# Loading wq in four transfers of spaced rows, and other cuts of wo, in a decode kernel

## The chip, the cores and the metric

The kernel runs on one core of a Trainium2 chip. Its time is the device time of one execution in microseconds (us); the median of several executions is given. A profile is one execution taken by the hardware profiler.

## The reference

One token passes through grouped-query attention over a long cache and through a SwiGLU block, and a gate mixes the two. All inputs are bf16.

```python
# x [1,1,512]; wq [512,4096]; wo [4096,512]; K and V [1,8,32768,128]; w_gate, w_up [512,1792]; w_down [1792,512]
g = sigmoid((x * gate_w).sum(-1, keepdims=True))
q = (x @ wq)                                   # 32 heads of 128, four heads share one of the 8 K/V heads
p = softmax((q @ k^T) * 128 ** -0.5)           # over 32768 positions
a = (p @ v) @ wo
b = (silu(x @ w_gate) * (x @ w_up)) @ w_down
out = g * a + (1 - g) * b
```

K and V are 64 MB each, so 148 MB are read for very little arithmetic.

## The kernel before

All loads are issued by the sync engine (SP) on one queue, in an order written out by hand: wq, then the rows x and gate_w, w_gate, w_up, then K and V head by head into five pages of SBUF as they come free, then w_down, and last wo. Sixteen DMA engines serve that queue.

**wq** (line 307) comes as one transfer. Partition p of the page `PG_Q` receives rows 4p to 4p+3 of wq, which lie together in memory: 32 KB a partition, 128 partitions. (In this document "a row of wq" is one such 32 KB row of a partition.) TensorE waits for it (line 458, `sem_q` at 16) and then multiplies x with it.

**K and V** are streamed by a loop over the 8 K/V heads. TensorE transposes pieces of K into PSUM (`emit_fill`, line 337), VectorE copies them to SBUF, TensorE makes scores (line 349), ScalarE takes exponentials, and TensorE multiplies with V (line 406). SP waits for pages to come free before it issues the next load.

**wo** (lines 325 to 329) comes in five transfers. Partition p receives 32 rows of wo, and a "row block" j is the j-th of these on all partitions (1 KB a partition, 128 KB in all). `WO_CUTS` says which row blocks a transfer brings: 16, 8, 4, 2 and 2.

**The end** has two ways to multiply with a row block. `emit_strip` makes one matmul of 512 columns into one of four PSUM rows of `ps_c`. Four such partial rows must later be added: ScalarE copies `ps_c` to SBUF as `part` (line 763), and TensorE adds its four rows with the selecting vector `sel4` in fp32 (line 760). `emit_rows` makes four matmuls of 128 columns, straight into the final place `ps_d`. Row blocks below `WO_ROWS` (24) go by strips, on top of the strips of w_down; the others go by rows. The first piece of wo is used inside `emit_end` (line 557); the other four and the sum stand in the loop at lines 756 to 760. VectorE then casts the result (line 765) and SP stores it (line 768).

Of the kernel before, what the change touches and what calls it, by code (L numbers as in the profile page):

```python
# [12 lines left out]
def bass_gated_mix__gqa_block_cached__swiglu_ffn__decode_kernel(  # L13
# [16 lines left out]
    DH = A_k_cache.shape[3]  # L30
    H = A_wq.shape[1] // DH
# [5 lines left out]
    KC = D // 128  # L37
# [13 lines left out]
    LAG = 2  # L51
    STEP = 16
    WOJ = H * DH // 128
    SCALE = float(DH) ** -0.5
    assert UPG == STEP and UPP % NKT == 0 and UPP % NST == 0
    assert KC * H * DH <= PAGE and 2 * KC * F <= PAGE and WOJ * NOUT <= PAGE
    WO_CUTS = [0, 16, 24, 28, 30, 32]
    WO_ROWS = 24
    OC = NOUT // 128
    FS = F // 4  # L60

# [10 lines left out]
    PG_Q = PG_V  # L72
# [5 lines left out]
    with ExitStack() as es:  # L78
        def S_(name):
            return es.enter_context(nc.semaphore(name))  # L80
# [5 lines left out]
        sem_q = S_("s_q")  # L86
        sem_f = S_("s_f")
        sem_wo = [S_(f"s_wo{i}") for i in range(len(WO_CUTS) - 1)]
        sem_ld_x = S_("s_ld_x")
# [42 lines left out]
        sem_part = S_("s_part")  # L132
# [4 lines left out]
        def T(name, shape, dt):  # L137
            return es.enter_context(nc.sbuf_tensor(name, shape, dt))
# [11 lines left out]
        sel4 = T("sel4", [128, 16], FP32)  # L150
# [7 lines left out]
        page = T("page", [128, NPG, PAGE], BF16)  # L158
# [12 lines left out]
        oTs = T("oTs", [128, H], BF16)  # L171
        O2a = T("O2a", [128, WOJ], BF16)
        O2 = T("O2", [128, WOJ], BF16)
        res_row = T("res_row", [128, 128], BF16)
# [14 lines left out]
        M_O0 = M_T0 + FC  # L189
        M_X0 = M_O0 + WOJ  # L190
        M_G0 = M_X0 + KC
# [16 lines left out]
        part = acc[:, :, :].rearrange("p q d -> p (q d)")  # L208

        def vrows(pg):  # L210
            return page[:, pg, :].rearrange("p (r d) -> p r d", d=DH)

        wq_v = page[:, PG_Q, 0 : KC * H * DH].rearrange("p (c n) -> p c n", c=KC)
        wgu = page[:, PG_F, 0 : 2 * KC * F].rearrange("p (w c f) -> p w c f", w=2, c=KC)
        wo_v = page[:, PG_X, 0 : WOJ * NOUT].rearrange("p (j n) -> p j n", j=WOJ)
        qall = qblk[:, :].rearrange("p (g e c) -> p g e c", e=2, c=2 * HPG)

        def emit_strip(pe, w, vec, j, start, stop):
            c = j % NSTRIP
            return pe.matmul(  # L220
                ps_c[32 * c : 32 * c + 1, :],
                vec[:, j : j + 1],
                w[:, j, :],
                start=start,
                stop=stop,
                skip_group_check=True,
            )

        def emit_rows(pe, lhsT, rhs, start, stop):
            for oc in range(OC):  # L230
                ins = pe.matmul(  # L231
                    ps_d[32 * oc : 32 * oc + 1, :],
                    lhsT,
                    rhs[:, oc * 128 : (oc + 1) * 128],
                    start=start,
                    stop=stop,
                    skip_group_check=True,
                )
            return ins

        def emit_wo(pe, k):
            pe.wait_ge(sem_wo[k], 16)
            for j in range(WO_CUTS[k], WO_CUTS[k + 1]):
                if j < WO_ROWS:
                    ins = emit_strip(pe, wo_v, O2, j, False, j >= WO_ROWS - NSTRIP)
                else:
                    ins = emit_rows(
                        pe, O2[:, j : j + 1], wo_v[:, j, :], j == WO_ROWS, j == WOJ - 1
                    )
            if WO_CUTS[k + 1] == WO_ROWS:  # L250
                ins.then_inc(sem_pe_part, 1)
            return ins
# [4 lines left out]
        with nc.Block("main") as block:  # L257
# [12 lines left out]
            @block.sync  # L270
            def _(sp):
                def load_k(g):
                    lo = PG_A if g % 2 else PG_B
                    dst = page[:, lo : lo + NB, :].rearrange("p b (r d) -> p b r d", d=DH)
                    src = A_k_cache[0, g, :, :].rearrange("(p b r) d -> p b r d", b=NB, r=R)
                    if g > 1:
                        sp.wait_ge(sem_fill, UPG * (g - 1) + UPP)
                        sp.dma_start(
                            dst.rearrange("p b r d -> p (b r d)"),
                            src.rearrange("p b r d -> p (b r d)"),  # L280
                        ).then_inc(sem_k[0], 16)
                        return
                    for b in range(NB):
                        first = lo + b == PG_B
                        if g and first:
                            sp.wait_ge(sem_fill, UPP)
                        sp.dma_start(dst[:, b, :, :], src[:, b, :, :]).then_inc(
                            sem_k[0] if first else sem_k1 if g else sem_k[1], 16
                        )

                def load_v(g):
                    src = A_v_cache[0, g, :, :].rearrange("(p b r) d -> p b r d", b=NB, r=R)
                    if g < G - 1:
                        if g:
                            sp.wait_ge(sem_v_free, STEP * (g + 1))
                        else:
                            sp.wait_ge(sem_pe_h, 1)
                        sp.dma_start(
                            page[:, PG_V : PG_V + NB, :].rearrange("p b n -> p (b n)"),
                            src.rearrange("p b r d -> p (b r d)"),  # L300
                        ).then_inc(sem_v, 16)
                        return
                    for b in range(NB):
                        sp.wait_ge(sem_fill, UPG * (G - 1 + b))
                        sp.dma_start(vrows(PG_L[b]), src[:, b, :, :]).then_inc(sem_vl[b], 16)

                sp.dma_start(wq_v, A_wq.rearrange("(p c) n -> p c n", c=KC)).then_inc(sem_q, 16)  # L307
                sp.dma_start(x_row[0:1, :], A_x[0, :, :]).then_inc(sem_ld_x, 16)  # L308
                sp.dma_start(gw_row[0:1, :], gate_w.unsqueeze(0)).then_inc(sem_ld_g, 16)
                for w, src in enumerate((B_w_gate, B_w_up)):  # L310
                    sp.dma_start(  # L311
                        wgu[:, w, :, :], src.rearrange("(p c) f -> p c f", c=KC)
                    ).then_inc(sem_f, 16)
                load_k(0)
                for g in range(1, G):
                    load_k(g)
                    if g == 2:
                        sp.wait_ge(sem_ident, 2)
                        sp.dma_start(out_rows, ident[SEL, :]).then_inc(sem_out, 16)
                    load_v(g - 1)  # L320
                load_v(G - 1)
                sp.dma_start(
                    wd[:, :, :], B_w_down.rearrange("(p j) n -> p j n", j=FC)
                ).then_inc(sem_ld_wd, 16)
                sp.wait_ge(sem_v_free, STEP * G)
                src = A_wo.rearrange("(p j) n -> p j n", j=WOJ)
                for k, s in enumerate(sem_wo):
                    a, b = WO_CUTS[k], WO_CUTS[k + 1]
                    sp.dma_start(wo_v[:, a:b, :], src[:, a:b, :]).then_inc(s, 16)  # L329

            @block.tensor
            def _(pe):
# [103 lines left out]
                def emit_start():  # L436
# [18 lines left out]
                    ins.then_inc(sem_pe_x, 1)  # L455
                    pe.wait_ge(sem_pz, 2)
                    pe.wait_ge(sem_dve_x, 1)
                    pe.wait_ge(sem_q, 16)
                    for t in range(QT):
                        for c in range(KC):  # L460
                            for k in range(NSTRIP):
                                n = (t * NSTRIP + k) * QN
# [60 lines left out]
                    for n, sem in enumerate((sem_v_free, sem_red)):  # L523
                        c = M_P0 + HPG * n
# [34 lines left out]
                with pe.Fori(0, 2, 1) as turn:  # L559
                    with pe.If(turn > 0):  # L560
                        emit_end()
                    with pe.If(turn < 1):
                        emit_start()

            @block.scalar
            def _(act):
# [10 lines left out]
                with act.Fori(0, G * STEP, STEP) as i:  # L577
# [5 lines left out]
                    for b in range(NB):  # L583
                        bank = R - odd if b else odd
                        for h in range(HPG):
# [4 lines left out]
                                bias=nbias[:, h : h + 1],  # L590
                                scale=SCALE,
                                accum_out=esum[:, b, h : h + 1],
# [5 lines left out]
            def _(dve):  # L598
# [108 lines left out]
                with dve.Fori(0, G * STEP, STEP) as i:  # L707
                    for n in range(UPG + 1):
# [28 lines left out]
                    dve.tensor_scalar(  # L737
                        nbias[:, :], ps_m[:, M_B0 : M_B0 + HPG], -SCALE, None, op0=ALU.mult
                    ).then_inc(sem_nbias, STEP)
# [13 lines left out]
                dve.tensor_copy(O2[:, :], ps_m[:, M_O0 : M_O0 + WOJ]).then_inc(sem_dve_O2, 1)  # L753

        pe, act, dve, sp = nc.tensor, nc.scalar, nc.vector, nc.sync
        for k in range(1, len(sem_wo)):
            ins = emit_wo(pe, k)
            if WO_CUTS[k] == WO_ROWS:
                pe.wait_ge(sem_part, 1)
                emit_rows(pe, sel4[:, 0:1], part, False, False)  # L760
        ins.then_inc(sem_pe_sum, 1)
        act.wait_ge(sem_pe_part, 1)
        act.activation(part, ps_c, ACT.Copy).then_inc(sem_part, 1)
# [34 lines left out]
```

## Time and profile before

| | before |
|---|---|
| median of 3 runs | 351.08 us (350.98 to 351.13) |
| the profiled execution | 351.06 us, of which its span is 349.7 us |
| mean granted TensorE clock | 0.838 |
| PE (matmuls) busy | 259.8 us, 74% of the span |
| VectorE busy | 186.9 us, 53% |
| ScalarE busy | 33.4 us, 10% |
| DMA, share of 16 engines | 98.4% |
| DMA, mean rate | 424 GB/s for 148.22 MB |

The span runs from the first to the last instruction of the core; the time of an execution is a little longer. Engines are named PE (TensorE matmuls), PEld (its weight loads), DVE (VectorE), ACT (ScalarE), POOL (GpSimd) and SP; SPq is SP's DMA queue. A share of busy time is an average over stages with different limits, so it only says where to look. A line of the profile such as `L307` names a line of the kernel before.

### The profile page before, as it was taken

What the parts mean: (1) busy time and instruction counts of PE and PEld (TensorE: products, weight loads), DVE (VectorE), ACT (ScalarE), POOL (GpSimd) and SP (SyncE); (2) the same over time, 40 slices, a digit from 0 to 9 for tenths busy, and PEclk for the clock granted to TensorE, in tenths of its full rate; (3) what the DMA queues carried; (4) which work ended last, traced back from release to release, by engine and by line L of the source; (5) the groups of instructions that cost most, each with busy time, mean ns of one, the idle gap of its engine ahead of it and who ended that gap; (6) DMA issues with size and microseconds to landing.
All of it is one profiled execution on the core that took longest, in us unless ns stands there. A gap on an engine that the chain in (4) does not pass through costs nothing.

```text
span 349.7 us, 8785 instructions
## 1 busy us (share of the span) xinstructions
PE 259.8 (74%) x3891; PEld 217.9 (62%) x3891; DVE 186.9 (53%) x236; ACT 33.4 (10%) x143; POOL 0.4 (0%) x6
## 2 busy tenths in 40 slices
PE   1355993899649970999669992999179983999485
PEld 1124993898349950997369942996179843995231
DVE  4144994698129920697139910994149811893110
ACT  1002000300210003000210003000300003000400
POOL 0000000000000000000000000000000000000000
PEclk9975998799859995799659986999659975998875
DMA  8999999999999999999999999999999999999995
GB/s 320 429 449 420 433 423 453 452 412 435 457 405 450 412 442 465 412 427 442 412 465 412 427 442 427 450 412 435 472 405 435 442 412 465 412 397 435 421 420 216
DMA packets 4059, 148.22 MB, mean 424 GB/s; under 512 B 466, under 2 KB 468, under 8 KB 852
## 3 DMA queue, kind: packets, MB, share of 16 engines
q1 hardware_dynamic: 4052, 148.12, 98.4%
q8 instruction: 6, 0.10, 0.1%
q14 instruction: 1, 0.01, 0.0%
HBM read 148.11 MB, written 0.00 MB: 423 GB/s over the span
## 4 chain that ended last, share of the span: by engine, by line
DMA 61%; PE 34%; issue 2%; DVE 1%; SPq 1%; DVEq 0%
DMA page<-in_A_k_cache_dram 55%; PE pst L337 25%; PE ps_sc L349 6%; DMA page<-in_A_wo_dram 6%; PE ps_o L406 2%; DVE ktT L711 1%; PE ps_sc L231 0%; SPq L311 0%; SPq L329 0%; DVE pmaxf L719 0%; PE ps_m L390 0%; PE ps_m L386 0%; SPq L307 0%; SPq L308 0%; DVE res_row L765 0%
## 5 line engine op out<-in xcount | busy, mean ns | idle before, releaser
L711 DVE COPY ktT<-pst 128x2048 bf16<-128x2048 bf16 x128 | 153.1, 1221 | 65.2 <-PE pst L337 61.0
L337 PE MATMUL pst<-ident_f,page 128*128 128x128 f32 x1024 | 145.9, 296 | 41.2 <-DMA page<-in_A_k_cache_dram 39.6
L337 PEld LDWEIGHTS pst<-ident_f,page 128*128 128x128 f32 x1024 | 124.3, 153 | 45.9 <-DMA page<-in_A_k_cache_dram 40.3
L349 PE MATMUL ps_sc<-qcur,ktT 128*128 128x8 bf16 x2048 | 64.1, 166 | 6.4 <-DVE ktT L711 6.4
L349 PEld LDWEIGHTS ps_sc<-qcur,ktT 128*128 128x128 bf16 x2048 | 63.7, 96 | 8.1 <-DVE ktT L711 7.1
L406 PE MATMUL ps_o<-page,ET 128*16 128x512 bf16 x512 | 38.4, 467 | 3.5 <-ACT ET L586 3.5
L406 PEld LDWEIGHTS ps_o<-page,ET 128*16 128x16 bf16 x512 | 14.3, 105 | 23.9 <-issue 12.2
L586 ACT ACTIVATE ET<-ps_sc,nbias 128x128 bf16 x64 | 23.9, 555 | 52.2 <-DVE nbias L737 52.2
L579 ACT ACTIVATE acc<-ps_o 128x512 f32<-128x512 f32 x8 | 4.8, 597 | 221.3 <-PE ps_o L406 217.3
L729 DVE TENSOR_REDUCE gm<-ps_m 4x1 f32<-4x128 f32 x8 | 2.2, 279 | 40.8 <-PE ps_m L386 40.8
L586 ACT ACTIVATION_READ_ACCUMULATOR ET<-ps_sc,nbias 128x1 f32 x64 | 18.2, 285 | 0.0
L719 DVE TENSOR_REDUCE pmaxf<-ps_sc 128x4 f32<-128x512 f32 x16 | 11.0, 686 | 8.4 <-PE ps_sc L349 8.4
L427 PE MATMUL ps_m<-sel,acc 128*128 128x4 f32 x64 | 8.4, 255 | 1.8 <-ACT acc L579 1.6
L427 PEld LDWEIGHTS ps_m<-sel,acc 128*128 128x128 f32 x64 | 7.7, 191 | 2.5 <-ACT acc L579 2.2
L390 PE MATMUL ps_m<-diag,ones_f 4*128 4x4 f32 x16 | 4.0, 315 | 6.9 <-DVE diag L733 6.9
L390 PEld LDWEIGHTS ps_m<-diag,ones_f 4*128 4x128 f32 x16 | 3.5, 270 | 8.4 <-issue 8.4
L696 DVE RECIPROCAL rS<-ps_m 128x4 f32<-128x4 f32 x9 | 1.6, 183 | 11.0 <-PE ps_m L427 11.0
L448 PE MATMUL ps_m<-ones_bf,x_row 1*128 1x1 bf16 x4 | 0.3, 172 | 9.3 <-DMA x_row<-in_A_x_dram 9.3
L418 PEld LDWEIGHTS ps_m<-esum,ones_f 128*128 128x128 f32 x32 | 4.2, 190 | 3.5 <-issue 3.5
L448 PEld LDWEIGHTS ps_m<-ones_bf,x_row 1*128 1x128 bf16 x4 | 0.2, 114 | 9.6 <-DMA x_row<-in_A_x_dram 9.6
L220 PE MATMUL ps_sc<-page,O 128*1 128x512 bf16 x24 | 2.7, 592 | 3.3 <-DMA page<-in_A_wo_dram 3.3
L418 PE MATMUL ps_m<-esum,ones_f 128*128 128x4 f32 x32 | 4.9, 258 | 0.0
(70 smaller groups left out, 52.5 us busy)
## 6 DMA issues: line engine op xcount, KB each, us to landing
page<-in_A_k_cache_dram SPq DMA_DIRECT2D x4, 4096.0 KB, 34.3
page<-in_A_v_cache_dram SPq DMA_DIRECT2D x2, 4096.0 KB, 27.2
page<-in_A_wq_dram SPq DMA_DIRECT2D x1, 4096.0 KB, 13.5
page<-in_A_wo_dram SPq DMA_DIRECT2D x1, 2048.0 KB, 18.5
page<-in_B_w_gate_dram SPq DMA_DIRECT2D x1, 1792.0 KB, 16.7
page<-in_B_w_up_dram SPq DMA_DIRECT2D x1, 1792.0 KB, 20.6
wd<-in_B_w_down_dram SPq DMA_DIRECT2D x1, 1792.0 KB, 21.0
page<-in_A_wo_dram SPq DMA_DIRECT2D x1, 1024.0 KB, 20.7
```

Source lines behind the costliest of these rows:

```text
L220: return pe.matmul(ps_c[32 * c : 32 * c + 1, :], vec[:, j : j + 1], w[:, j, :], start=start, stop=stop, skip_group_check=True,)
L337: ins = pe.transpose(pst[u % NST][:, k * 128 : (k + 1) * 128], kv[:, n * 128 : (n + 1) * 128], ident_f[:, :],)
L349: ins = pe.matmul(ps_sc[b][:, col : col + 2 * HPG], kt[:, k, e, :], qcur[:, e, :], start=(e == 0), stop=(e == 1),)
L390: pe.matmul(ps_m[:, M_B0 : M_B0 + HPG], ones_f[0:HPG, :], diag[:, :], start=True, stop=True,).then_inc(sem_b, STEP)
L406: ins = pe.matmul(ps_o[32 * c : 32 * c + RQ * HPG, :], ET[:, n : n + RQ, :].rearrange("p n h -> p (n h)"), v[:, k * RQ : (k + 1) * RQ, :], ...
L418: pe.matmul(ps_m[:, M_S0 : M_S0 + HPG], ones_f[:, :], esum[:, b, :], start=(b == 0), stop=(b == NB - 1),)
L427: ins = pe.matmul(ps_m[:, M_P0 : M_P0 + HPG], acc[:, q, :], sel4[:, q * HPG : (q + 1) * HPG], start=(q == 0), stop=(q == RQ - 1),)
L579: act.activation(part, ps_o[:, :], ACT.Copy).then_inc(sem_acc, STEP)
L586: act.activation(ET[:, b * R : (b + 1) * R, h], sc[:, h, bass.ds(bank, R)], ACT.Exp, bias=nbias[:, h : h + 1], scale=SCALE, accum_out=esum ...
L711: dve.tensor_copy(ktT[:, n % NKT, :], pst[n % NST][:, :].bitcast(BF16)).then_inc(sem_cp, 1)
L719: dve.tensor_reduce(pmaxf[:, b, :], sc, AX.X, ALU.max).then_inc(sem_d, 1)
L729: dve.tensor_reduce(gm[:, :], ps_m[0:HPG, M_A0 : M_A0 + 128], AX.X, ALU.max).then_inc(sem_d, STEP - 2)
```

## The change

wq is no longer one transfer but four on the same queue: the first takes every 8th row from row 0, the second every 8th row from row 4, the third every 4th row from row 2, the fourth every 2nd row from row 1. These are 16, 16, 32 and 64 rows of 32 KB. TensorE waits for all four. wo comes in pieces of 16, 9, 4, 2 and 1 row blocks. Only the first piece goes by strips; the sum of the four strips is placed ahead of the row matmuls of the other four pieces, and it is now the first matmul into `ps_d`.

```diff
-    WO_CUTS = [0, 16, 24, 28, 30, 32]
-    WO_ROWS = 24
+    WQ_ROWS = ((0, 8), (4, 8), (2, 4), (1, 2))
+    WO_CUTS = [0, 16, 25, 29, 31, 32]
+    WO_ROWS = WO_CUTS[1]
...
                     ins = emit_rows(
-                        pe, O2[:, j : j + 1], wo_v[:, j, :], j == WO_ROWS, j == WOJ - 1
+                        pe, O2[:, j : j + 1], wo_v[:, j, :], False, j == WOJ - 1
                     )
...
-                sp.dma_start(wq_v, A_wq.rearrange("(p c) n -> p c n", c=KC)).then_inc(sem_q, 16)
+                wq_d = page[:, PG_Q, 0 : KC * H * DH]
+                wq_s = A_wq.rearrange("(p c) n -> p (c n)", c=KC)
+                for first, step in WQ_ROWS:
+                    sp.dma_start(wq_d[first::step, :], wq_s[first::step, :]).then_inc(sem_q, 16)
...
-                    pe.wait_ge(sem_q, 16)
+                    pe.wait_ge(sem_q, 16 * len(WQ_ROWS))
...
         pe, act, dve, sp = nc.tensor, nc.scalar, nc.vector, nc.sync
+        pe.wait_ge(sem_part, 1)
+        emit_rows(pe, sel4[:, 0:1], part, True, False)
         for k in range(1, len(sem_wo)):
             ins = emit_wo(pe, k)
-            if WO_CUTS[k] == WO_ROWS:
-                pe.wait_ge(sem_part, 1)
-                emit_rows(pe, sel4[:, 0:1], part, False, False)
```

## The prediction

> **What bounds the kernel now.** I read the page first: its engine shares and 40 slices, then its DMA rows. After those came SP's timeline for the first 3 us, a table of short stages over the first 13 us, the timeline of the last 7 us, and the chain of waits.
>
> From the page, the DMA row of the 40 slices, the queue row, and the landing of wq:
>
> ```profile
> DMA  8999999999999999999999999999999999999995
> ...
> q1 hardware_dynamic: 4052, 148.12, 98.4%
> ...
> page<-in_A_wq_dram SPq DMA_DIRECT2D x1, 4096.0 KB, 13.5
> ```
>
> The sixteen DMA engines are at 98.4% of the span. PE is busy 74% of it, but the chain that ended last gives DMA 61%. Only the first slice (8) and the last (5) are open. Time can therefore be won or lost in three ways: the DMA engines start sooner or later, some transfer runs below the full rate, or the work behind the last landing changes. The full rate is the page's mean of 424 GB/s, 26.5 GB/s an engine. A row of wq is 4096 KB / 128 = 32 KB, so it takes an engine 32.8 KB / 26.5 = 1.24 us.
>
> The start, SP's timeline (start us, length us):
>
> ```profile
> 0.74 0.38 SPq L307 DMA_DIRECT2D page<-in_A_wq_dram  x1
> 1.18 0.31 SPq L308 DMA_DIRECT2D x_row<-in_A_x_dram  x1
> ```
>
> and the table of stages (the last number is GB/s; a packet is booked in the stage in which it starts, which is why a share can pass 1):
>
> ```profile
> 0.00:1.50 1.50, 0.00 (x0) 0.00 (x0) 0.57 (x5) 0.77 (x1) 0.44 (x6) 1.00 0.00 0
> 1.50:2.50 1.00, 0.00 (x0) 0.00 (x0) 0.86 (x6) 0.51 (x1) 0.00 (x0) 1.00 1.79 492
> 2.50:3.50 1.00, 0.98 (x4) 0.93 (x4) 0.71 (x2) 0.00 (x0) 0.00 (x0) 1.00 0.16 66
> 3.50:4.50 1.00, 0.24 (x2) 0.00 (x0) 0.84 (x2) 0.00 (x0) 0.00 (x0) 1.00 1.16 492
> ```
>
> 492 KB are 15 rows of wq. Fifteen engines began their first row in 1.5 to 2.5 us, and the next fifteen rows began in 3.5 to 4.5. The first row of each engine thus took about 2.0 us, not 1.24: the start loses some 0.75 us an engine beside the latency of the issue.
>
> The end, timeline (PE = matmuls, PEld = weight loads):
>
> ```profile
> 342.39 1.73 PE L220 MATMUL ps_sc<-page,O 128*1 128x512 bf16 x16 [2.61 <-DMA page<-in_A_wo_dram]
> 344.81 1.02 PE L220 MATMUL ps_sc<-page,O 128*1 128x512 bf16 x8 [0.69 <-DMA page<-in_A_wo_dram]
> 345.88 0.60 ACT L763 ACTIVATE acc<-ps_sc 128x512 f32<-128x512 f32 x1 [8.53 <-PE ps_sc L220]
> 346.08 0.60 PE L231 MATMUL ps_sc<-page,O 128*1 128x128 bf16 x16 [0.25 <-DMA page<-in_A_wo_dram]
> 346.53 0.61 PE L231 MATMUL ps_sc<-acc,sel 128*1 128x128 f32 x8
> 346.91 0.86 PE L231 MATMUL ps_sc<-page,O 128*1 128x128 bf16 x16
> 347.39 0.10 PEld L231 LDWEIGHTS ps_sc<-page,O 128*1 128x1 bf16 x8 [0.32 <-DMA page<-in_A_wo_dram]
> 347.82 0.29 DVE L765 CAST res_row<-ps_sc 128x128 bf16<-128x128 f32 x1 [7.82 <-PE ps_sc L231]
> 348.14 0.53 SPq L768 DMA_DIRECT2D out_dram<-res_row  x1
> ```
>
> Each of the five pieces of wo finds PE waiting. Behind the last landing (347.39) come eight matmuls, DVE's cast and the store.
>
> The profiled execution took 351.06 us: a span of 349.7 and 1.36 around it. The median of the runs is 351.08, so the sum is made against 351.06.
>
> **The change part by part: the end.** Pieces of 9, 4, 2, 1 row blocks replace 8, 4, 2, 2. The bytes and the number of transfers stay, so the last landing stays at 347.39. The three landings before it come one row block later: 128 KB / 424 = 0.3 us, to about 345.1, 346.4 and 347.0.
>
> PE after the change. The 16 strips end at 344.12. ACT copies for 0.60, until about 344.8. The sum (0.38 from its first start to the next group's) is done by 345.2. That is a new wait on ACT at this place, and all row matmuls of wo stand behind it; it is covered by the landing at 345.1 but for 0.1 us. The 9 blocks are 36 row matmuls. Sixteen of them took from 346.08 to 346.53, 28 ns apart, so 36 take 1.0 us, to 346.2, before the landing at 346.4. PE waits for every later piece, and 1.1 us of slack stand before 347.39. Without that slack the 32 more row matmuls would cost 32 x 28 ns = 0.9 us, and the eight strips that they replace would give back their 1.02 (344.81).
>
> Behind the last landing, 8 matmuls take 347.39 to 347.80. With 4 fewer starts of 28 ns the stretch is 0.3, a gain of 0.1 us. Packets of 1 KB in the last piece have no row at this place; with 8 an engine I put -0.1 to +0.1 us on them and take nothing. The 24 more matmuls (64 by rows and 16 by strips for 32 and 24) also lengthen PE's program. One more instruction packet (0.10 MB / 6 = 17 KB by the page's q8 row) would hold one engine 0.6 us; I take nothing, and it lies inside the range.
>
> **The start: issues and waits.** Three more issues on SP cost about 0.43 us each with their gaps (1.81 to 2.21 for w_gate). x_row, gw_row, w_gate, w_up and K are issued 1.3 us later. Their packets stand behind eight rows of wq an engine (x_row was waited for until 13.06), so that costs nothing. The second transfer is issued by 1.6 us and the fourth by 2.4, before an engine is through its first row. PE now waits for a count of 64 instead of 16; behind that wait stand all of its work on wq, the SwiGLU part and K, as before, and it ends with the same last row.
>
> **The start: the rate of the pieces.** This is the term that decides. Every transfer seen at 424 GB/s had all 128 rows. No row shows one of 16 rows, 8 partitions apart, one row an engine. Its bounds, per row and engine: 1.24 us if it flows like the rest, and below what before paid if a short transfer also starts sooner (down to -0.9 in all, see the gaining rival); and 2.48 us where two engines must take turns at one place in SBUF. The nearest row is before's own first sixteen rows, 2.0 us. I take the upper half for the two 16-row transfers: the first goes from 2.0 to 2.4 (+0.4), the second from 1.24 to 2.4 (+1.2). The transfers of 32 and 64 rows are nearer to the full one, and I let them flow. Less 0.1 for a shorter first issue and 0.1 at the end, the sum is +0.4 + 1.2 - 0.2 = +1.4 us: 351.06 + 1.4 = 352.5. Nothing later gives it back, because the queue has work in every slice.
>
> **Rivals.** *All eight rows take turns.* If two engines meet at one place in every row, each row costs up to 1.24 more. An engine with a lead over its partner shares only the rest of the row. The rows' starts lie within 1 us, so I take a lead of 0.15 us: 8 x (1.24 - 0.15) = +8.7, less the 0.2: 359.6 (5 to 9.5 for leads of 0.6 to 0.05). It decides if the sharing holds for the spaced rows of all four transfers. For it speaks that all four are spaced alike; against it, that no transfer in this trace runs at half rate.
>
> [...]
>
> *The start is repaired, faster.* If the 2.0 us of the first rows come from laying out 128 rows at once, 16 rows start at full rate. That gains the 0.75, some 0.15 of an issue shorter than 0.38, and 0.1 at the end: 350.1. It decides if the second rows begin before about 3.3 us. For it: fifteen engines begin within 1 us and then all lose the same. Against it: the loss may be the first reading of memory, which remains.
>
> *Nothing but the end.* The rows flow as before, or the chip splits 16 rows over fewer engines, so that the change does not do what it says and every engine still carries eight rows without a gap: -0.2, 350.9.
>
> **How the numbers follow.** The forecast has 0.33 (own range 351.8 to 354), all eight rows 0.26, the repaired start 0.24, nothing 0.17. A fifth of a per cent, 0.7 us, is about what a measurement of this kernel can tell from no change. So slower is 0.33 + 0.26 = 0.59, within 0.17, faster 0.24. The range runs from 350.0, near the repaired start, to 360.0, just over the eight-row case. What it leaves out is the upper end of that case and a start that gains more than 0.9, together under 0.2.
>
> **What would show it.** In the stages at the start: second rows beginning near 4.2 us and third rows near 6.6 for the forecast; before 3.3 us for the repaired start. wq's wait on PE (14.32 before) ends near 15.8 in the forecast, 23 with all eight rows, 13.4 with the repaired start. At the end, PE waits for each of the five pieces, the sum lies before 345.3, and from the last landing to DVE's cast it is 0.3 us. If PE's row matmuls run without a wait from 345 to the cast, my cover at the end is wrong. If time moves between 30 and 340 us rather than in the first 15, the whole account is wrong.

## The result, and the profile after

The changed kernel takes 353.72 us (median of 6 runs, 353.40 to 354.39) against 351.10 (350.98 to 351.29): a ratio of 1.0079 with a 95% interval of 1.0069 to 1.0089, 2.6 us more. Its profiled execution took 353.40 us, of which 352.0 are the span, 2.34 more than the profiled execution before.

From the page after: the DMA row of the 40 slices, the GB/s row below it, the queue row, and the landings of wq.

```profile
DMA  8999999999999999999999999999999999999995
GB/s 225 403 442 421 437 441 418 456 447 424 432 417 432 462 410 432 462 417 432 447 432 424 417 432 462 410 432 462 417 432 447 432 424 417 432 428 417 423 420 227
...
q1 hardware_dynamic: 4100, 148.12, 98.4%
...
page<-in_A_wq_dram SPq DMA_DIRECT2D x1, 2048.0 KB, 12.7
...
page<-in_A_wq_dram SPq DMA_DIRECT2D x2, 512.0 KB, 6.8
```

The DMA row of digits and the queue's share are the same as before, to the digit. The bytes are what tells: the first slice moved 225 GB/s where before it moved 320, as its page has it:

```profile
GB/s 320 429 449 420 433 423 453 452 412 435 457 405 450 412 442 465 412 427 442 412 465 412 427 442 427 450 412 435 472 405 435 442 412 465 412 397 435 421 420 216
```

That is 95 x 8.8 us = 0.84 MB less, or 2.0 us at 424 GB/s. The engines were "busy" all the same (8 tenths of the first slice in both): a packet counts as busy for as long as it takes, and a second row took 2.36 us where before it took 1.25.

The table of stages at the start, after (us, then PE, PEld, DVE, ACT, POOL, the clock, the DMA share and GB/s; a packet is booked where it starts, 32.8 KB each):

```profile
1.50:2.50 1.00, 0.00 (x0) 0.00 (x0) 0.86 (x6) 0.51 (x1) 0.00 (x0) 1.00 1.82 410
2.50:3.50 1.00, 0.98 (x4) 0.92 (x4) 0.71 (x2) 0.00 (x0) 0.00 (x0) 1.00 0.53 131
...
4.00:5.00 1.00, 0.00 (x0) 0.00 (x0) 1.00 (x2) 0.00 (x0) 0.00 (x0) 1.00 2.23 492
...
6.40:7.20 0.80, 0.00 (x0) 0.00 (x0) 0.00 (x0) 0.00 (x0) 0.00 (x0) 1.00 1.82 533
...
8.20:9.20 1.00, 0.00 (x0) 0.00 (x0) 0.00 (x0) 0.00 (x0) 0.00 (x0) 1.00 1.15 492
9.20:10.20 1.00, 0.00 (x0) 0.00 (x0) 0.00 (x0) 0.00 (x0) 0.00 (x0) 1.00 1.15 492
```

Twelve first rows and a 16 KB packet of instructions start in 1.5 to 2.5 (410 KB), fifteen second rows in 4.0 to 5.0 (492 KB), thirteen third rows in 6.4 to 7.2, fifteen fourth rows in 8.2 to 9.2 and the fifth in 9.2 to 10.2. The DMA share beside the 492 KB is 2.23 for the second rows and 1.15 for the fourth: the same bytes took 1.9 times as long. The trace also records the start and the length of every DMA packet. Sorted by start, the rows of wq fall into rounds of sixteen, one an engine; the means of a round are, in us:

| | start of the first rows | first rows took | second | third | fourth |
|---|---|---|---|---|---|
| before | 1.97 | 1.87 | 1.25 | 1.25 | 1.21 |
| after | 2.37 | 2.28 | 2.36 | 1.73 | 1.22 |

The differences add up to 2.4 us, beside the 2.34 measured: 0.40 of a later start, 0.41 and 1.11 in the first and second rows, 0.48 in the third.

SP's issues in the chain of waits after (start us, length us):

```profile
0.74 0.61 SPq L311
...
1.40 0.56 SPq L311
...
2.01 1.44 SPq L311
...
3.49 0.60 SPq L311
```

The first issue of spaced rows takes 0.61 us where the full wq took 0.38.

PE's wait for wq ends at 16.28, where before it ended at 14.32 and the forecast had 15.8:

```profile
16.28 3.58 PE L467 MATMUL pst<-page,xT 128*1 128x512 bf16 x32 [0.36 <-DMA page<-in_A_wq_dram]
```

The timeline of the end, after:

```profile
344.75 1.03 PE L221 MATMUL ps_sc<-page,O 128*1 128x512 bf16 x16 [1.67 <-DMA page<-in_A_wo_dram]
346.10 0.60 ACT L766 ACTIVATE acc<-ps_sc 128x512 f32<-128x512 f32 x1 [5.44 <-PEq L258]
346.75 0.60 PE L232 MATMUL ps_sc<-acc,sel 128*1 128x128 f32 x8 [0.96 <-ACT acc L766]
347.45 0.84 PEld L232 LDWEIGHTS ps_sc<-page,O 128*1 128x1 bf16 x36 [0.60 <-DMA page<-in_A_wo_dram]
348.72 0.31 PEld L232 LDWEIGHTS ps_sc<-page,O 128*1 128x1 bf16 x16 [0.43 <-DMA page<-in_A_wo_dram]
349.41 0.10 PEld L232 LDWEIGHTS ps_sc<-page,O 128*1 128x1 bf16 x8 [0.38 <-DMA page<-in_A_wo_dram]
349.74 0.09 PEld L232 LDWEIGHTS ps_sc<-page,O 128*1 128x1 bf16 x4 [0.23 <-DMA page<-in_A_wo_dram]
350.07 0.29 DVE L768 CAST res_row<-ps_sc 128x128 bf16<-128x128 f32 x1 [6.76 <-PE ps_sc L232]
```

PE waits for every piece of wo. The last landing moved from 347.39 to 349.74, 2.35 us, and from it to the cast are 0.33 us where before had 0.43. The loss is made before the end, and the end gives 0.1 back.

### The profile page after: what moved, and what is told of

Its sections match the earlier page's. It is cut to its first block, busy times and chain, and to the rows that moved or that the text cites. A ratio compares the mean times of both kernels' runs of the same rounds, so it can differ in the third digit from the quotient of the medians.

```text
span 352.0 us, 8836 instructions
## 1 busy us (share of the span) xinstructions
PE 262.7 (75%) x3915; PEld 220.7 (63%) x3915; DVE 187.1 (53%) x236; ACT 33.4 (9%) x143; POOL 0.4 (0%) x6
## 3 DMA queue, kind: packets, MB, share of 16 engines
q1 hardware_dynamic: 4100, 148.12, 98.4%
## 4 chain that ended last, share of the span: by engine, by line
DMA 66%; PE 31%; SPq 2%; issue 1%; DVE 0%
DMA page<-in_A_k_cache_dram 60%; PE pst L341 24%; DMA page<-in_A_wo_dram 6%; PE ps_sc L353 5%; PE ps_o L410 1%; SPq L311 1%; DVE ktT L715 0%; SPq L333 0%; SPq L315 0%; PE ps_sc L232 0%; SPq L312 0%; DVE res_row L768 0%; SPq L313 0%
## 5 line engine op out<-in xcount | busy, mean ns | idle before, releaser
L341 PE MATMUL pst<-ident_f,page 128*128 128x128 f32 x1024 | 147.5, 299 | 40.3 <-DMA page<-in_A_k_cache_dram 38.8
L341 PEld LDWEIGHTS pst<-ident_f,page 128*128 128x128 f32 x1024 | 126.1, 155 | 44.7 <-DMA page<-in_A_k_cache_dram 39.8
L410 PE MATMUL ps_o<-page,ET 128*16 128x512 bf16 x512 | 40.3, 485 | 3.5 <-ACT ET L590 3.5
```

The source lines that it names most:

```text
L341: ins = pe.transpose(pst[u % NST][:, k * 128 : (k + 1) * 128], kv[:, n * 128 : (n + 1) * 128], ident_f[:, :],)
L410: ins = pe.matmul(ps_o[32 * c : 32 * c + RQ * HPG, :], ET[:, n : n + RQ, :].rearrange("p n h -> p (n h)"), v[:, k * RQ : (k + 1) * RQ, :], ...
```

## The experiments

"Before" is run beside each; its median was 351.12, 351.18 and 351.24 us in the three jobs. All kernels but `wo_only` keep the end of before.

**The two halves apart.** `wq_only` is before with the four wq transfers, `wo_only` the changed kernel with wq in one.

```diff
 # wo_only, against the changed kernel
-                for first, step in WQ_ROWS:
-                    sp.dma_start(wq_d[first::step, :], wq_s[first::step, :]).then_inc(sem_q, 16)
+                sp.dma_start(wq_v, A_wq.rearrange("(p c) n -> p c n", c=KC)).then_inc(sem_q, 16)
...
-                    pe.wait_ge(sem_q, 16 * len(WQ_ROWS))
+                    pe.wait_ge(sem_q, 16)
```

> Only the four wq transfers of the change, the end as before. Theory A (two engines take turns in the two 16-row transfers): the whole loss is here, 353.4 to 354.0, and the table of stages shows second rows starting in 4 to 5 us and third rows in 6.4 to 7.2, as in the changed kernel. Theory B (the end does part of it: the longer run of row matmuls and the sum ahead of them): under 352.5.

Measured: 353.89 us, ratio 1.0074 (1.0059 to 1.0090). The whole loss is in wq.

> Only the wo pieces and the sum's new place, wq in one transfer. Theory A: the last landing stays, four matmuls fewer behind it, 351.0 (350.8 to 351.1), and 0.3 us from the last landing to the cast where before has 0.43. Theory B: slower than 351.4.

Measured: 350.99 us against 351.12, ratio 0.9999 (0.9990 to 1.0008). A gain of 0.1 us can't be told from none in the times, but its timeline has the step that was expected, 0.33 us from the last landing to the cast:

```profile
345.59 1.77 PEld L231 LDWEIGHTS ps_sc<-page,O 128*1 128x1 bf16 x60
...
347.59 0.09 PEld L231 LDWEIGHTS ps_sc<-page,O 128*1 128x1 bf16 x4 [0.23 <-DMA page<-in_A_wo_dram]
347.92 0.29 DVE L764 CAST res_row<-ps_sc 128x128 bf16<-128x128 f32 x1 [8.26 <-PE ps_sc L231]
```

The first line shows something else: 60 weight loads of row matmuls run from 345.59 without a wait, so here PE waits only for the first and the last piece of wo. 0.23 us of waiting are left, where the prediction had 1.1 us of slack.

**Splitting wq without the 16-row transfers.** `wq_columns` has four transfers of all 128 rows; `wq_32_32_64` has three spaced ones, the first of 32 rows.

```diff
 # wq_columns
-    WQ_ROWS = ((0, 8), (4, 8), (2, 4), (1, 2))
+    WQ_PARTS = 4
...
-                for first, step in WQ_ROWS:
-                    sp.dma_start(wq_d[first::step, :], wq_s[first::step, :]).then_inc(sem_q, 16)
+                wq_n = KC * H * DH // WQ_PARTS
+                for k in range(WQ_PARTS):
+                    cut = slice(k * wq_n, (k + 1) * wq_n)
+                    sp.dma_start(wq_d[:, cut], wq_s[:, cut]).then_inc(sem_q, 16)
...
-                    pe.wait_ge(sem_q, 16 * len(WQ_ROWS))
+                    pe.wait_ge(sem_q, 16 * WQ_PARTS)
 # wq_32_32_64
-    WQ_ROWS = ((0, 8), (4, 8), (2, 4), (1, 2))
+    WQ_ROWS = ((0, 4), (2, 4), (1, 2))
```

> wq in four transfers again, but each with all 128 rows and 8 KB of each row. Theory A: the number of transfers costs nothing, 350.9 to 351.4. Theory C (four issues or four completions of a split wq cost the time): as the change, 353 or more.

Measured: 351.12 us, ratio 0.9999 (0.9990 to 1.0009). Four transfers cost nothing as such.

> wq_only with three transfers, every 4th row from 0, every 4th from 2, every 2nd from 1 (32, 32, 64 rows): no transfer with a single row an engine. Theory A with turns in the 16-row transfers alone: the two slow rows are gone, 351.1 to 352.0, what is left being the later start of the first packet (0.4 us) and the slow start that before has too. Theory A with turns in all spaced transfers: at least as slow as the change, above 353.4. Theory B (any spaced or split wq starts slowly): 352.5 to 353.7.

Measured: 351.47 us, ratio 1.0008 (0.9999 to 1.0018). Its table of stages:

```profile
1.50:2.50 1.00, 0.00 (x0) 0.00 (x0) 0.86 (x6) 0.51 (x1) 0.00 (x0) 1.00 1.39 377
...
3.50:4.50 1.00, 0.24 (x2) 0.00 (x0) 0.84 (x2) 0.00 (x0) 0.00 (x0) 1.00 1.15 492
...
5.10:5.70 0.60, 0.00 (x0) 0.00 (x0) 0.52 (x3) 0.00 (x0) 0.00 (x0) 1.00 1.93 819
...
6.40:7.00 0.60, 0.00 (x0) 0.00 (x0) 0.00 (x0) 0.00 (x0) 0.00 (x0) 1.00 1.94 819
```

Fifteen rows (492 KB, or 819 x 0.6) start around 4.0, 5.4 and 6.7. The share of 1.15 over 16 engines and 15 rows makes 1.2 us a row from the second on. Rows 4 and 2 partitions apart flow at the full rate. What is left, about 0.35 us by the medians, goes with the later first packet: by the packet records the first rows start 0.5 us later than before and take 0.1 less.

**Is it one row an engine, or where the rows lie?** `wq_adjacent` takes rows 0 to 15, 16 to 31, 32 to 63, 64 to 127. `wq_middle` begins with four transfers of 16 rows, every 4th from 32, 33, 34 and 35, and ends with the blocks 0 to 31 and 96 to 127.

```diff
-    WQ_ROWS = ((0, 8), (4, 8), (2, 4), (1, 2))
+    WQ_ROWS = ((32, 96, 4), (33, 96, 4), (34, 96, 4), (35, 96, 4), (0, 32, 1), (96, 128, 1))   # wq_middle
...
-                for first, step in WQ_ROWS:
-                    sp.dma_start(wq_d[first::step, :], wq_s[first::step, :]).then_inc(sem_q, 16)
+                for lo, hi, step in WQ_ROWS:
+                    sp.dma_start(wq_d[lo:hi:step, :], wq_s[lo:hi:step, :]).then_inc(sem_q, 16)
```

> wq in transfers of 16, 16, 32 and 64 adjacent rows (0 to 15, 16 to 31, 32 to 63, 64 to 127), the end as before. [...] Theory E (a transfer with one row an engine is slow by itself, wherever the rows lie): rows 1 and 2 at 2.4 us as in the change, 353 to 354.5 in all. [...]

Measured, one run: 365.46 us, 14.3 more than before. The table of stages has the first rows starting in 1.5 to 2.5, the second in 5 to 6, the third in 9.5 to 11:

```profile
1.50:2.50 1.00, 0.00 (x0) 0.00 (x0) 0.86 (x6) 0.51 (x1) 0.00 (x0) 1.00 3.68 524
...
5.00:6.00 1.00, 0.00 (x0) 0.00 (x0) 0.58 (x4) 0.00 (x0) 0.00 (x0) 1.00 4.46 508
...
9.50:11.00 1.50, 0.00 (x0) 0.00 (x0) 0.00 (x0) 0.00 (x0) 0.00 (x0) 1.00 2.06 328
```

By the shares, the first rows took 3.7 us each (3.68 x 16 over 16 rows) and the second 4.6. This is still one row an engine, so theory E falls: the number of rows is not the cause.

> wq in four transfers of 16 rows, every 4th from 32, 33, 34 and 35 (to 95), then rows 0 to 31 and 96 to 127, the end as before. Theory E (one row an engine is slow by itself): rows 1 to 4 at 2.4 us each. Theory A: it depends on where the 16 rows lie, not on their number; if these sixteen are at sixteen different places, rows 1 to 4 take 1.2 to 1.3 us after the start, and the two blocks of 32 adjacent rows are the slow ones (2.4 a row), 355 to 357 in all. [...]

Measured, one run: 358.82 us, 7.6 more. That is above the 355 to 357 expected of theory A. The stages say where:

```profile
1.50:2.50 1.00, 0.00 (x0) 0.00 (x0) 0.86 (x6) 0.51 (x1) 0.00 (x0) 1.00 1.70 475
...
3.50:4.50 1.00, 0.24 (x2) 0.00 (x0) 0.84 (x2) 0.00 (x0) 0.00 (x0) 1.00 1.14 492
4.50:5.50 1.00, 0.00 (x0) 0.00 (x0) 0.97 (x5) 0.00 (x0) 0.00 (x0) 1.00 0.94 393
...
6.20:7.20 1.00, 0.00 (x0) 0.00 (x0) 0.00 (x0) 0.00 (x0) 0.00 (x0) 1.00 1.58 492
...
11.20:17.00 5.80, 0.00 (x0) 0.00 (x0) 0.00 (x0) 0.00 (x0) 0.00 (x0) 1.00 0.96 203
```

The sixteen-row transfers flow here: the second rows start around 4.0 and 492 and 393 GB/s follow, with shares of 1.14 and 0.94, 1.2 us a row. Only the fourth rows, the last ahead of the blocks, are slowed (share 1.58, 1.7 us a row). The blocks of 32 adjacent rows then run at 203 GB/s, half the rate, and the loss is larger than the 4.8 that four rows at 2.4 explain. The packet records have most of the rest: 0.4 of a later start, 0.5 in the fourth rows and 0.9 in the packets of w_gate behind the blocks, which with 5.0 in the blocks' four rows make 6.8 of the 7.6. The same kind of transfer, 16 rows with one row an engine, therefore ran at full, half or near a quarter of the rate by the rows it took: 1.2 us a row here, 2.36 in the changed kernel, 4.6 in `wq_adjacent`.

**Dose.** `wq_four_16` cuts the 32-row transfer into two of 16 rows, every 8th from 2 and from 6: `WQ_ROWS = ((0, 8), (4, 8), (2, 8), (6, 8), (1, 2))`.

> wq_only with the 32-row transfer cut into two of 16 rows, every 8th from 2 and every 8th from 6: four slow rows instead of two. Theory A: two more rows at 2.4 for 1.2 us, 356.0 to 356.8. Theory F (the loss is one fixed start-up of the spaced transfers, however many rows): 353.5 to 354.2.

Measured: 355.98 us, ratio 1.0130 (1.0109 to 1.0150). That is 4.7 us more than before, where `wq_only` had 2.8: two more slow rows cost about 2.0 us, 1.0 each, just below the 356.0 to 356.8 of theory A. By the packet records rows two, three and four took 2.4 us each, and the fifth, the first behind the 16-row transfers, 1.9.

**Place in the order.** `wq_reversed` has 64, 32, 16, 16 rows: `((1, 2), (2, 4), (4, 8), (0, 8))`. `wq_16_inside` has 64, 16, 16, 32: `((1, 2), (0, 8), (4, 8), (2, 4))`.

> The change's four wq transfers in the opposite order: 64, 32, 16, 16 rows, the end as before. Theory A (turns in the 16-row transfers): the two slow rows come last, +1.2 each, and the start is like before's with a first packet 0.3 us later: 353.2 to 354.0. Theory D (the loss belongs to the first two rows of the kernel, whatever transfer brings them): 351.1 to 351.8, with rows 7 and 8 at 1.2 us.

Measured: 355.91 us, ratio 1.0129 (1.0112 to 1.0146). Theory D falls: the slow rows go with the transfer and not with the start. But the loss is twice what theory A gave. The profiled execution is the longest of the four (357.42 us). The wait of PE for wq in its timeline ends at 20.50, where the changed kernel has 16.28:

```profile
20.50 3.49 PE L467 MATMUL pst<-page,xT 128*1 128x512 bf16 x32 [4.29 <-DMA page<-in_A_wq_dram]
```

> The change's four wq transfers in the order 64, 16, 16, 32 rows, the end as before. wq_reversed cost 4.7 us instead of the 2.4 that two slow rows explain, and there the packets of w_gate behind the last 16 rows were slow too. Theory G (the extra 2.3 comes from the 16-row transfers standing right ahead of a full one): here a 32-row transfer stands between, 353.2 to 354.2. Theory H (16 rows late in wq cost twice as much anyway): 355.3 or more.

Measured: 355.11 us, ratio 1.0108 (1.0087 to 1.0129), 3.9 more than before, between the two theories: neither is borne out. PE's wait for wq ends at 18.18. Behind other rows the two 16-row transfers cost 3.9, ahead of a full transfer 4.7, and as the first thing 2.8. One part is visible: the kernel's very first row is slow in before too (1.9 us), so a 16-row transfer there loses only the rest (2.28 in the changed kernel). The packet records place more of it. In `wq_reversed` the two slow rows took 2.3 and 2.4 us, as theory A has it, but the packets of w_gate right behind them lost another 1.4 us an engine, and the first start was 0.45 later; with the 2.3 us that wq's rows lost in all, that is about 4.1 of the 4.7. In `wq_16_inside` the loss behind falls on wq's own 32-row transfer, whose first row took 1.8 us; start and rows make 3.1 of the 3.9. Why the packets behind lose more right ahead of a full transfer stays open. PE's wait tells less than it seems: in the profile of `wq_reversed` fifteen engines end their last row of wq by 15.8 us and one at 19.27, the one that had first brought a packet of instructions (3.07 to 3.95), if a packet that starts as another ends is on the same engine.

## Why the prediction was right, and where its sizes were off

**The deciding term held, in kind and in size.** The two 16-row transfers ran at about half rate: their rows took 2.28 and 2.36 us (2.4 predicted) against the 1.22 of the fourth rows. That two engines take turns at one place was the author's estimate of why, sized as twice the 1.24 of a row; no run shows two engines meeting. Without 16-row transfers (`wq_32_32_64`, `wq_columns`) all or nearly all of the loss is gone, and with four of them it grows by 2.0. That the spaced transfers of 32 and 64 rows flow was right as well: `wq_32_32_64` shows 1.2 us a row. But the reason given for it, that they are nearer to the full transfer, does not hold, so this part was luck: in `wq_adjacent` the 64 adjacent rows took about 2.5 us each by the packet records. What counts in these runs is which rows a transfer takes, and not how many: 16 rows took 1.2, 2.36 or 4.6 us each, 64 rows 1.2 or 2.5.

**Which rows are slow, and what is not shown.** Every 8th row ran at about half rate (2.36 us a row), every 4th from 32 at full rate (1.2 us, but 1.7 in the last such transfer ahead of the blocks), a block of 32 adjacent rows at half rate (203 GB/s), and 16 adjacent rows took 3.7 and 4.6 us a row. That blocks of adjacent rows would be the slow ones was expected of theory A before any run showed it; `wq_adjacent` and `wq_middle` then did. The rival that all eight rows take turns did not come true: from the fourth row on the changed kernel takes 1.22 us a row. No trace here names the rows of an engine. One rival is not excluded by a run: every kernel reads row p of wq into partition p, so the place in SBUF always changed together with the place in memory. That SBUF is the place is not shown.

**The size was short by 0.9 us** (+1.4 predicted, +2.34 between the two profiled executions). Two terms of the sum were mis-sized, by 0.5 us each:

- *Issue, -0.1.* I took a transfer of fewer rows for a shorter issue. The first issue of spaced rows takes 0.61 us, not 0.38, and twelve rows instead of fifteen have started by 2.5 us; the first rows start 0.40 later on average. `wq_32_32_64` prices this at about +0.35. It is also why second and third rows begin near 4.65 and 7.0 us, and not near 4.2 and 6.6. In `wq_adjacent`, whose rows are not spaced, SP's first issue took 0.39 again:

```profile
0.73 0.39 SPq L311
```

- *Third row, 0.* I let the 32-row transfer flow from its first row. Behind a 16-row transfer its first row takes 1.73 us, 0.5 more than before, while the same transfer in second place in `wq_32_32_64` has no such row (1.2 us). So it is an after-effect of the 16-row transfers and not a cost of its own.

*The two slow rows, +1.6*, had the size predicted: +0.41 (0.4 predicted) and +1.11 (1.2 predicted) by the table of rounds.

**The repaired start** fell. In `wq_middle` the first transfer has 16 rows of a kind that flows (1.2 us each in the transfers behind it), and still the second rows start around 4.0 as in before (492 GB/s in 3.5 to 4.5 in both) and not before 3.3: the slow first rows are not from laying out 128 rows at once.

**SP's queue.** I had the fourth transfer issued by 2.4 us; it was issued by 4.1, since one issue took 1.44. As predicted of x_row and the rest, this cost nothing that shows: the fourth transfer's rows follow four others.

**The end** was right in its time, within 0.1 us: the same last landing in `wo_only` but for 0.2 (347.59), and 0.33 us instead of 0.43 behind it. The cover was weaker than predicted. In the changed kernel PE waits for all five pieces. The new wait on ACT was longer than I had it, since ACT starts 0.3 us after the strips end (345.78 to 346.10), released by PE's queue at the end of the block and not by the strips alone; the wait for the second piece (0.60 us of PE idle until 347.45) covers it, as the prediction had it. In `wo_only` that wait is gone and the row matmuls run through to the last piece, nearly the sign that the prediction named for a wrong cover. It cost nothing because the last landing was still 0.23 us later than PE. The time moved in the first 15 us, where it was looked for.

## What to carry to other kernels

In these runs a transfer of some of the rows had a rate of its own, full, half or near a quarter (1.2, 2.36 and 4.6 us a row), by which rows it took. Its engines read as busy at every rate (98.4% of the span before and after), so compare GB/s (320 and 225 in the first slice) and not the busy share. Before a load is cut into pieces, ask which rows, and so which partitions, each piece takes: cutting the columns (all 128 rows in each piece) cost nothing here (351.12 us for both), cutting rows at a spacing of 8 cost about 1 us for each row an engine (2.0 us for two more in `wq_four_16`). In this kernel, whose DMA engines are at 98.4% of the span, the early loss was not made up later: 2.0 us were lost in the first 9 us, and the last landing came 2.35 later.

## What the runs showed of the hardware that was not expected

- The issue of spaced rows took longer: 0.61 and 0.56 us for the first two of the changed kernel, against 0.39 and 0.40 in `wq_adjacent`, which has the same row counts without spacing.
- One issue on SP that began near 2.0 us took 1.44 us in the changed kernel, and nothing that shows waited for it. A packet of instructions was on its way from 2.01 to 3.11. In `wq_only` that packet took 1.97 us and the issue 2.35; in `wq_four_16` the packet came only at 2.78, and the issue that began at 2.01 took 0.59. This points to SP waiting for the packet; no run tests it.
- The cost of two 16-row transfers differed by what is ahead of and behind them: 2.8 us at the head of wq, 3.9 inside, 4.7 at its end.
- A slow first row, 1.8 to 1.9 us on average, was there with three different first transfers: 128 rows (before, 1.87), 32 spaced rows (`wq_32_32_64`), or 16 rows of a kind that flows afterwards (`wq_middle`). An engine that began its first row only at 2.84 us took 1.21 for it (before), and so did one at 3.03 in `wq_middle`, so the slow stretch seems to belong to the time and not to an engine's first row.
